# Fifteen tiles at the end of a fused cross network in another order, and the sixth group's output turned tile by tile

## The chip, the core and the metric

The kernel runs on one core of a Trainium2 chip. The metric is the device time of one execution in microseconds (us). Before the change the median of 3 runs was 473.92 us (473.2 to 474.08).

## The reference

A cross network of six layers over rows of 416 features (`B, F, D, L = 16384, 26, 16, 6`, all in bfloat16):

```python
x = x0
for l in range(L):
    proj = jnp.einsum('bd,de->be', x, ws[l]) + bs[l]
    x = x0 * proj + x
return x
```

Each layer is a 16384 x 416 by 416 x 416 product, a bias, a multiplication by the first input and an addition of the layer's own input. A row's layers depend on one another, the rows don't.

## The kernel before

**Groups, jobs, tiles, chunks.** The 16384 rows are cut into 8 groups (0 to 7) of 2048 rows. A job `(g, l)` is layer `l` of group `g`. Activations lie transposed, features on partitions: three full tiles of 128 features (`t` or `i` = 0, 1, 2) and a tail of 32. An output tile `((g, l), i)` has four chunks of 512 rows (`j` = 0 to 3). A chunk is 13 matmuls: on each of the four 32-row groups of the TensorE array one for each of the three input tiles, and one more for the 32 tail features on one of the row groups. A tile is so 52 matmuls of 32 x 128 weights over 512 columns (lines 1065 and 1069). The 32 tail features of the output of two or three jobs are computed together in a tail batch (`tails`, lines 689 and 677). Every chunk sums in a PSUM bank of its own, of which there are eight.

**Evacuation.** ScalarE adds the bias and writes the chunk to `tw` (line 551); for each pair of chunks VectorE multiplies by the first input (563) and adds the layer's input (568). The tail batch goes through lines 605 to 613. An addition is held back behind the next multiplication.

**Order.** `order` lists the 48 jobs; its last six are (5,5), (6,4), (7,3), (6,5), (7,4), (7,5). From the tenth job on nearly everything on TensorE is placed by a table, `ORDER`: `replay` reads it letter by letter, each letter naming one of the four row groups and which of the chunks begun lately it works on next, and `|` placing a tail batch. The table fits one order of tiles: with another order of tiles the whole table is a new one. `tiles` gives the order of tiles, and `where` after which tile a tail batch comes.

Called by their jobs, the last fifteen tiles that the table places are those of e5 = (5,5), d6 = (6,4), d7 = (7,3), e6 = (6,5) and e7 = (7,4). Before the change they stand so: e5 0, 1, 2; d6 0, 1, 2; d7 0, 1, 2; e6 0, 1; e7 0; e6 2; e7 1, 2. e6 needs d6, e7 needs d7. A tail batch for e5, d6 and d7 comes after d6 0, and one for e6 and e7 after e6 1; the planner may put either a little later.

**The last job** (7,5), "natural" in the code, is computed with the rows on partitions: 16 blocks of 128 rows, four at a time (`kk` = 0 to 3, in each of them `j` = 0 to 3), each with three matmuls over 128 features (line 1130), two small ones for tail and bias (1013, 1019), a copy by ScalarE (1176), a multiplication (1182) and an addition (1188) by VectorE, and a store (1195). The addition needs the layer's input, the output of e7, with the rows on partitions. It comes there in three ways: tile 0 and tile 1 by DMA transposes (`rest_turn`, line 935, tile 1 in two halves), tile 2 by TensorE transposes (`turn_last`, line 1141, two of them with a pair of chunks each) and copies (1150), the tail by TensorE (1155) and ScalarE (1163).

**Output of the other groups.** A group's output is turned into one buffer, `ost`, by DMA transposes (three tiles and the tail), then stored (line 923). There is only one `ost`: the turns of a group wait until the store of the group before has read it. All of these DMAs, the transposes of `rest_turn` and the small rotations of the tails (445, 446) are issued by SyncE, in the order of the program: one that waits holds up all behind it. Group 5 (the sixth) is turned by `turn(g, 0)` in `tails`, then, once all of e5 and its tail are done, by `turn_rest`, `turn(g, 1)` and `turn(g, 2)` in `output` (890, 897). Group 6 is turned tile by tile, each as soon as it is written (`turn_out`, 903, called in `finish_tile`); its tail's turn comes with the tail batch, its tail's copy into `ost` is ScalarE's (914), its two stores come late in the program.

Of the kernel before, what the change touches and what calls it, by code (L numbers as in the profile page):

```python
# [21 lines left out]
class Program:  # L22
# [179 lines left out]
READ, NEXT, BACK, SECOND, PAIR, TAILS, SUMS = 19, 56, 70, 92, 56, 220, 240  # L202
LETTERS = "ABCDEFGHIJKLMNOPQRSTUVWXYZabcdefghijklmnopqrstuvwxyz0123456789"
ORDER = (
    "ABCDMBCTNaELBaUfBWIfZSUHhKQPBCMTVIDSJATKBQLWBQXKNALCZQLWBQCbMRLWBITWBATWZMLCVYLSBQLCRbICRAPaJUeH"
    "N|AWPJQGDQBDWNITCJnQCZTIWBLQWNALWBQXCNIDWZIDWJYTCJbMWHRIODBMSBfICVDMSVIDSJAbeJMXCJgXSBQLOZDIWNTA"
    "CNTUBOQDNaTAJaDQZKXMSBPYCNbICVLQaBTIWNALWNQDKBAbWNITCBcPSIZDKRYXCRIPeBIXaNQLG|ABWPAVKPQBCPBUaPAN"
    "WbQdKHMVSDBQOXBMKXAVSLMBCPZQCPJAWfJQaHMVSDBQOXBMKXAVSLMBCPZAWPJAWfJYCLUZOTANaLUBSXNE|KDBUORDIDSB"
    "MfSBYfKRMXGAdPWAVKPQBaLQBTKNADOZTAaNAXKNYDWYJPCJbUCVTIBeQLBaTINWHAVODUKBXQKBLAVaQLGBAfWZATWJYPGA"
    "VPYBWPANWLYRCLBQWDNSLAJaQfBSMZLGQXBSI|CDVMCXBMeXQBKPAVeLMBafMVKTAhSLYNHCBQXBSMLBaAOXZQKHMVSDBQOX"  # L210
    "BMCbMVDOVISDBMeXANKfYROHAZWPANKfQBSLYNDKNAXCNQWDNAWbNISDYBSPUBKfMVCfMVSLEBaTMVCP|IBWLAVCXMRCPANe"
    "XYBKPVQaHNAaPBMbKRASLYNHCBQXNCMLWBAaPQVCLQBaTNIGfVQODNAPaJAXKQBLSBAOXYBWPQZCLZQOXFISDAVSDQNCfINS"
    "XBAXSNYGDAZSXINHeBYTCNYSLEBSfMVCP|IBWLAVCXMRCPANeXYBKPVQaHNAaPBMbKRASLYNHCBQXBSIPBaIDZSIDSZAbJSM"
    "XCJgXOBIWPBUKPAdWLMBKDZQXBOIDaVQLOBIbCVbQKNEDWBQWPBMCbMVDOVISDBUeTMJGXAVOfIRCLQBaTN|ECPBWAPBYOXB"
    "ULadAXSZMLGRDYSBQbKNALWBQXKBQDOZIDVaITOBIbOBAbORcHKVATWMJHCUBXCMRLWAJTWMBPKAZLCBYPeQJXGARPWIZHCQ"
    "BTaN|ECPBWAPBYOXBUPadQDOZIXSMBPKVALSBQbCNAPWZAXSJPYWBPUCNULSBITOZALWBUTCNQLCZAXaNQLWFATWARPKUBDO"
    "YBXaMJTCIZDSIZXOQFDaARXCQNXCINDaUJPCANebQBSLZMGXBUiTN|ECPVSALBUCXNQCPJAeZXAWTJMaHBYORDYKNTACNfQW"
    "BPISBbISNDYKPVAKXBQWLBQXKNALCZQWLBQCbNAWPJAeLUZSDQJObAJXOYBLOVAXKBULCVQKDRIaXFAWPBUOLRAKbNQCDNQW"
    "DJMSXFAOTBASPZUCPJUSjF|ASPVIGDBYDaNITCJQbOVEDWMBXCMRDaMJXSEBDWAdXSIBfSVYLOBIXORALORYDKBQXCMRDaJM"
    "XSBIPSVALCRUbKBQLWBITWNEDCZTUKBITWBIDaRULOBAbSdMLGBUbSJE|ODVPAKBYDWRIDSJAfSBcbKNQXGZAPWBUPKRALaB"  # L220
    "UTCNQLCZITWMBPWJADOVAXeNITGBYTCRYLWARDaNQXKBITWNALOBYXCNQLCZITWBQLWBITWBQLOVADOQZXCNITWFATOBYPKR"
    "ALaNQDCNQXKFATWBQPWBAPSZULGBAbWNQDOdYTWFM|BCTMXBWMLBWAPdWQKDJAWfIZODYJOXAJXOYBLOVAXKNQHCBQWDMRCb"
    "BMaTVICLBYWfJAXeQZKHVMSDBQOXANKXAVSLMBCPYRKXABaPQVHKARXaIBLCVYLSNEXCMBWPIBWLAVCXMBWPAdKXYNGDMVaT"
    "JACXYNeTJ|EODBTAOBcOXBUPeZQKHVASXIBKTAZLSUBCXNQCPIZWDQJWDIRWPEBfCURbOEBPWAVKPQBCPQVaLENCXBQWPANW"
    "LAVCXQBSPYBaLAZWLMRGbIBSXAdSLYNHCBQXBSIPBaIDZSIDSZIXBScXJO|AXKRMDCNQDaNITGBQbBaITBaQLVOALOVAXOBU"
    "PKBUDVOITGBDUeBQXOdEbJWM|RCLASXBMSDNYKTBAOXQZCLMRCbINeTUFOLABaPAVKPQBCPVAOXRAePJAaXcJOHURKPQFCDO"
    "TAB"
)


# [76 lines left out]
def bass_standalone__cross_network_dcn__recsys_kernel(  # L307
# [24 lines left out]
    batches = []  # L332
# [336 lines left out]
    def tails(batch, corners_last=False, banks=None):  # L669
        bs_ = banks or take(len(batch))  # L670

        def corners():
            for (g, l), b in zip(batch, bs_):
                s3, tok3 = x3_src(g, l)
                for j in range(NJ):
                    (ri, qi), (ro, qo) = quad(g, l, j), quad(g, l + 1, j)
                    add("pe", lambda h, l=l, b=b, s3=s3, ri=ri, qi=qi, ro=ro, qo=qo: h.matmul(  # L677
                        psum[qo, b * CH:(b + 1) * CH], w3[l][qi, NT * P:D], s3[qi, :],
                        start=not corners_last, stop=corners_last, tile_position=(ri * T32, ro * T32)),
                        reads=tok3 + [("w3", l, ri)], writes=[("ps", b)])  # L680

        if not corners_last:
            corners()
        for (g, l), b in zip(batch, bs_):
            src, stok = x_src(g, l)
            for t in range(NT):
                for j in range(NJ):
                    ro, qo = quad(g, l + 1, j)
                    add("pe", lambda h, t=t, j=j, src=src, l=l, b=b, ro=ro, qo=qo: h.matmul(  # L689
                        psum[qo, b * CH:(b + 1) * CH], wm[l][:, t, NT * P:D], src(t, j, j + 1),  # L690
                        start=(corners_last and t == 0), stop=(not corners_last and t == NT - 1),
                        tile_position=(0, ro * T32)),
                        reads=[stok(t, j), wm_tok(l, NT)], writes=[("ps", b)])
            if not corners_last:
                evacuate_tail(g, l, b)
        if corners_last:
            corners()
            for k in sorted(range(len(batch)), key=lambda k: k != 1):
                evacuate_tail(*batch[k], bs_[k], vector=k == 1)
                while behind_tail:  # L700
                    behind_tail.pop(0)()
        pr.flush()
        for g, l in batch:
            if (g, l) == (LAST - 2, L - 1):
                turn(g, 0)
        for g, l in batch:
            if corners_last:
                prefill(g, l + 1)
                filled.add((g, l + 1))
        for g, l in batch:  # L710
            if (g, l) == (LAST - 1, L - 1):
                turn_rest(g)
            done_with(g, l)
        while later:
            load_group(later.pop(0))
# [158 lines left out]
    def output(g):  # L874

        s, s3 = xset[(g, L)], xtail[(g, L)]
        if g < LAST - 1:
            if g < LAST - 2:
                turn(g, 0)
            turn_rest(g)  # L880
            spread("pool")
            turn(g, 1)
            turn(g, 2)
            store(g, 0, NJ)
        free_x.append(s)
        free_3.append(s3)

    def turn(g, t):
        s = xset[(g, L)]
        add("sp", lambda h: h.dma_start_transpose(  # L890
            ost[:, :, t * P:(t + 1) * P], xs[s][:, t * GC:(t + 1) * GC]),
            reads=[("x", s, t, j) for j in range(NJ)], writes=[("ost", t, j) for j in range(NJ)],
            lane="ot" if t else "ot0", batch=g)

    def turn_rest(g):
        s3 = xtail[(g, L)]
        add("sp", lambda h: h.dma_start_transpose(ot3[:, :, :], x3s[s3][:, :]),
            reads=[("x3", s3)], writes=["ot3"], lane="ot3", batch=g)

    def turn_out(g, t):  # L900
        s = xset[(g, L)]
        for j0, j1 in ((0, NJ),) if t < NT - 1 else ((0, 2), (2, NJ)):
            add("sp", lambda h, j0=j0, j1=j1: h.dma_start_transpose(  # L903
                ost[:, j0 * KK:j1 * KK, t * P:(t + 1) * P], xs[s][:, t * GC + j0 * CH:t * GC + j1 * CH]),
                reads=[("x", s, t, j) for j in range(j0, j1)], writes=[("ost", t, j) for j in range(j0, j1)],
                lane=f"ot_{t}{j0}", batch=g)
# [32 lines left out]

    items = []  # L940
    where = {(b[0 if b in batches[4:-3] else min(1, len(b) - 1)], 0): b for b in batches[:-1]}
    where[((LAST - 1, L - 1), 1)] = batches[-1]
    del where[((0, 0), 0)]
    where[((0, 1), 0)] = where.pop(((1, 0), 0))
    tiles = [((1, 0), 0), ((1, 0), 1), ((0, 1), 0), ((0, 1), 1), ((0, 1), 2), ((1, 0), 2)]
    tiles += [(jb, i) for jb in order[3:-3] for i in range(NT)]
    end6, end7 = order[-3:-1]
    tiles += [(end6, 0), (end6, 1), (end7, 0), (end6, 2), (end7, 1), (end7, 2)]
    for jb, i in tiles:
        items.append(("tile", jb, i))  # L950
        if (jb, i) in where:
# [167 lines left out]
    g, l = LAST, L - 1  # L1119
# [155 lines left out]
```

## Time and profile before

| | us |
|---|---|
| median of 3 runs | 473.92 |
| profiled execution | 473.04 |
| its span on the core | 471.2 |
| TensorE busy in the span | 457.5 |
| VectorE busy | 403.3 |
| ScalarE busy | 380.7 |

A row of a timeline or of the chain begins with the start and the length in us from the span's start; then come the engine (PE is TensorE's matmuls, PEld its weight loads, DVE VectorE, ACT ScalarE, POOL GpSimd, SPq the DMA queue that SyncE issues to), the line of the kernel, the operation, output and input, and how many were merged in the row. Square brackets hold the idle time before it and what ended that.

### The profile page before, as it was taken

To read this page: it belongs to the slowest core of one execution; us is meant where nothing else is said; L and a number is where in the kernel's file an instruction comes from. 1 tells how busy PE (TensorE), PEld (TensorE's weight loads), DVE (VectorE), ACT (ScalarE), POOL (GpSimd) and SP (SyncE) were. 2 spreads that over 40 slices of the span, in tenths; PEclk is the share of its full clock that TensorE was granted. 3 is DMA by queue.
4 is the path that set the end of the run, shared out by engine and by line. 5 is a ranking of instruction groups with operands and counts; after the bars stand their busy time and mean duration, and the time that the engine had idled before them with its cause. 6 is when DMAs were issued, how large, how long until landed. Compare 5 with 4: busy or idle time off the path is not lost.

```text
span 471.2 us, 17812 instructions
## 1 busy us (share of the span) xinstructions
PE 457.5 (97%) x7997; PEld 264.1 (56%) x8001; DVE 403.3 (86%) x696; ACT 380.7 (81%) x609; POOL 5.5 (1%) x15
## 2 busy tenths in 40 slices
PE   9999999999999999999999999999999999999990
PEld 5444656565555567555655656566665555555540
DVE  2897899889889899798989898888988989988956
ACT  4686888887988889798888888788898888887870
POOL 1000000000000000000000000000000000000000
PEclk9999999999999999999999999999999999999996
DMA  8986969000003939094488975940000490306799
GB/s 230 180 184 141 153 110 190 4 25 7 21 2 55 187 113 189 15 153 152 70 155 155 219 141 110 218 154 3 24 4 3 89 224 16 70 2 126 195 182 295
DMA packets 139088, 53.78 MB, mean 114 GB/s; under 512 B 112762, under 2 KB 138500, under 8 KB 139012
## 3 DMA queue, kind: packets, MB, share of 16 engines
q1 hardware_dynamic: 138856, 52.54, 52.8%
q8 instruction: 62, 1.02, 0.9%
q10 hardware_dynamic: 156, 0.11, 0.1%
q14 instruction: 14, 0.11, 0.1%
HBM read 5.97 MB, written 13.63 MB: 42 GB/s over the span
## 4 chain that ended last, share of the span: by engine, by line
PE 93%; DVE 4%; SPq 1%; DMA 1%; ACT 1%; issue 0%; DVEq 0%
PE ps L1065 71%; PE ps L689 7%; PE ps L1069 6%; PE ps L642 4%; PE ps L636 1%; PE ps L677 1%; DVE tw L563 1%; DVE x L1182 1%; DVE x L1188 1%; DVE x L568 1%; PE ps L769 1%; DMA x<-x 1%; ACT tw L551 1%; PE ps L787 1%; PE ps L663 1%; SPq L903 0%
## 5 line engine op out<-in xcount | busy, mean ns | idle before, releaser
L1065 PE MATMUL ps<-x,wm 32*128 32x512 bf16 x6288 | 372.4, 374 | 0.0
L551 ACT ACTIVATE tw<-ps,bias 128x512 bf16<-128x512 f32 x524 | 326.1, 687 | 50.2 <-PE ps L1065 39.2
L1065 PEld LDWEIGHTS ps<-x,wm 32*128 32x128 bf16 x6288 | 220.8, 92 | 136.0 <-ACT tw L551 6.1
L563 DVE TENSOR_TENSOR tw<-tw,x 128x1024 bf16<-128x1024 bf16 x262 | 176.6, 690 | 42.2 <-ACT tw L551 41.1
L568 DVE TENSOR_TENSOR x<-tw,x 128x1024 bf16<-128x1024 bf16 x262 | 170.2, 685 | 0.3
L1069 PE MATMUL ps<-x,w 32*128 32x512 bf16 x524 | 158.2, 374 | 0.0
L1069 PEld LDWEIGHTS ps<-x,w 32*128 32x128 bf16 x524 | 44.4, 92 | 6.9
L689 PE MATMUL ps<-x,wm 128*32 128x512 bf16 x564 | 33.6, 380 | 0.0
L609 ACT ACTIVATE ts<-ps,bias 128x512 bf16<-128x512 f32 x32 | 20.4, 685 | 12.4 <-PE ps L677 12.4
L515 ACT ACTIVATE tw<-ps,bias 128x1024 bf16<-128x1024 f32 (+1 forms) x24 | 20.7, 937 | 8.2 <-PE ps L663 7.0
L689 PEld LDWEIGHTS ps<-x,wm 128*32 128x32 bf16 x564 | 13.5, 96 | 18.3 <-ACT tw L551 3.7
L642 PE MATMUL ps<-x,wm 128*128 128x512 bf16 x88 | 20.4, 379 | 0.7 <-issue 0.5
L613 DVE TENSOR_TENSOR x<-ts,x 128x512 bf16<-128x512 bf16 x47 | 18.5, 418 | 0.4
L524 DVE TENSOR_TENSOR tw<-tw,x 128x1024 bf16<-128x1024 bf16 (+1 forms) x21 | 13.0, 636 | 2.2 <-ACT tw L515 2.1
L642 PEld LDWEIGHTS ps<-x,wm 128*128 128x128 bf16 x92 | 8.3, 97 | 11.4 <-issue 2.1
L605 DVE SCALAR_TENSOR_TENSOR ts<-ps,bias,x 128x512 bf16<-128x512 f32 x15 | 11.2, 746 | 2.5 <-PE ps L677 2.4
L611 DVE TENSOR_TENSOR ts<-ts,x 128x512 bf16<-128x512 bf16 x32 | 12.7, 416 | 0.0
L529 DVE TENSOR_TENSOR x<-tw,x 128x1024 bf16<-128x1024 bf16 (+1 forms) x21 | 12.6, 633 | 0.0
L1188 DVE TENSOR_TENSOR x<-x,x 128x832 bf16<-128x832 bf16 (+1 forms) x9 | 4.8, 542 | 6.5 <-DMA x<-x 6.3
L1130 PE MATMUL ps<-wm,x 128*128 128x416 bf16 x48 | 9.7, 340 | 0.0
L1176 ACT ACTIVATE x<-ps 128x416 bf16<-128x416 f32 x16 | 7.6, 518 | 1.8 <-PE ps L1130 1.7
L797 DVE COPY x<-ps 128x512 bf16<-128x512 bf16 x5 | 2.0, 422 | 8.2 <-PE ps L787 8.2
(50 smaller groups left out, 70.6 us busy)
## 6 DMA issues: line engine op xcount, KB each, us to landing
out_dram<-ost SPq DMA_DIRECT2D x6, 1664.0 KB, 7.5
x<-x SPq DMA_DIRECT2D x24, 96.0 KB, 2.1
x<-in_x_dram SPq DMA_DIRECT2D x8, 208.0 KB, 4.2
x<-in_x_dram SPq DMA_DIRECT2D x4, 416.0 KB, 8.2
out_dram<-ost SPq DMA_DIRECT2D x2, 832.0 KB, 5.3
wm<-in_ws_dram SPq DMA_DIRECT2D x5, 312.0 KB, 3.4
x<-x SPq DMA_DIRECT2D x22, 64.0 KB, 2.0
out_dram<-x SPq DMA_DIRECT2D x3, 416.0 KB, 4.7
```

The source lines that it names most:

```text
L515: add("act", lambda h, a=a, w=w, b0=b0: h.activation(tw[r][:, a * CH:(a + w) * CH], psum[:, b0 * CH:(b0 + w) * CH], ACT_F.Identity, bias=b ...
L524: add("dve", lambda h, a=a, e=e: h.tensor_tensor(tw[r][:, a * CH:e * CH], tw[r][:, a * CH:e * CH], x0s[s0][:, i * GC + a * CH:i * GC + e * ...
L551: add("act", lambda h: h.activation(tw[r][:, j * CH:(j + 1) * CH], bank(b), ACT_F.Identity, bias=bias[:, i, l:l + 1], scale=1.0), reads=[( ...
L563: add("dve", lambda h: h.tensor_tensor(tw[r][:, o], tw[r][:, o], x0s[s0][:, c], ALU.mult), reads=[("tw", r, k) for k in both] + [x0_tok(s0 ...
L568: add("dve", lambda h: h.tensor_tensor(xs[so][:, c], tw[r][:, o], src(i, a, a + 2), ALU.add), reads=[("tw", r, k) for k in both] + [stok(i ...
L609: add("act", lambda h: h.activation(ts[r][:, :], bank(b), ACT_F.Identity, bias=bias[:, 3, l:l + 1], scale=1.0), reads=[("ps", b), "bias"], ...
L611: add("dve", lambda h: h.tensor_tensor(ts[r][:, :], ts[r][:, :], x03, ALU.mult), reads=[("ts", r)] + tok0, writes=[("ts", r)], release=True)
L613: add("dve", lambda h: h.tensor_tensor(x3s[so][:, :], ts[r][:, :], res, ALU.add), reads=[("ts", r)] + rtok, writes=[("x3", so), ("x3", so, ...
L642: add("pe", lambda h, t=t, j=j: h.matmul(bank(banks[j]), wm[l][:, t, ecols], src(t, j, j + 1), start=(first and t == 0), stop=(not first a ...
L689: add("pe", lambda h, t=t, j=j, src=src, l=l, b=b, ro=ro, qo=qo: h.matmul(psum[qo, b * CH:(b + 1) * CH], wm[l][:, t, NT * P:D], src(t, j, ...
L1065: add("pe", lambda h, l=l, t=t, j=j, b=b, q=q, ecols=ecols, src=src, kw=kw: h.matmul(bank(b), wm[l][q, t, ecols], src(t, j, j + 1)[q, :], ...
L1069: add("pe", lambda h, l=l, b=b, q=q, ecols=ecols, s3=s3, kw=kw: h.matmul(bank(b), w3[l][q, ecols], s3[q, :], **kw), reads=tok3 + [("w3", l ...
```

## The change

The order of the last fifteen tiles, the place of the last tail batch, the way in which group 5's output is turned, and the table. The new order of tiles is e5 0; d6 0, 1, 2; e5 1, 2; e6 0; d7 0, 1, 2; e6 1, 2; e7 0, 1, 2. The last tail batch is listed after e6 2, the one before it still after d6 0.

```diff
 ORDER = (
-    "ABCDMBCTNaELBaUfBWIfZSUHhKQPBCMTVIDSJATKBQLWBQXKNALCZQLWBQCbMRLWBITWBATWZMLCVYLSBQLCRbICRAPaJUeH"
...
+    "ABCDMBCTNaELRWMDdCYPJWEfNSIjCJUDSJATKBQLCRIXCRULOBAPaRXICRDYOJTUGBAXaBXQCdTIOVHCcRPUCNXISBDUiRPI"
...
         pr.flush()
         for g, l in batch:
-            if (g, l) == (LAST - 2, L - 1):
-                turn(g, 0)
-        for g, l in batch:
             if corners_last:
                 prefill(g, l + 1)
                 filled.add((g, l + 1))
         for g, l in batch:
-            if (g, l) == (LAST - 1, L - 1):
+            if l == L - 1 and g > LAST - 3:
                 turn_rest(g)
             done_with(g, l)
...
         if g < LAST - 1:
             if g < LAST - 2:
                 turn(g, 0)
-            turn_rest(g)
+                turn_rest(g)
             spread("pool")
-            turn(g, 1)
-            turn(g, 2)
+            if g < LAST - 2:
+                turn(g, 1)
+                turn(g, 2)
             store(g, 0, NJ)
...
     def turn_out(g, t):
         s = xset[(g, L)]
-        for j0, j1 in ((0, NJ),) if t < NT - 1 else ((0, 2), (2, NJ)):
+        for j0, j1 in ((0, NJ),) if t < NT - 1 or g < LAST - 1 else ((0, 2), (2, NJ)):
...
-    where[((LAST - 1, L - 1), 1)] = batches[-1]
+    where[((LAST - 1, L - 1), 2)] = batches[-1]
...
-    tiles += [(jb, i) for jb in order[3:-3] for i in range(NT)]
-    end6, end7 = order[-3:-1]
-    tiles += [(end6, 0), (end6, 1), (end7, 0), (end6, 2), (end7, 1), (end7, 2)]
+    tiles += [(jb, i) for jb in order[3:-6] for i in range(NT)]
+    e5, d6, d7, e6, e7 = order[-6:-1]
+    tiles += [(e5, 0), (d6, 0), (d6, 1), (d6, 2), (e5, 1), (e5, 2), (e6, 0), (d7, 0), (d7, 1), (d7, 2),
+              (e6, 1), (e6, 2), (e7, 0), (e7, 1), (e7, 2)]
...
     def finish_tile(g, l, n=1, i=0):
         tiles_done[(g, l)] = tiles_done.get((g, l), 0) + n
-        if (g, l) == (LAST - 1, L - 1):
+        if l == L - 1 and g > LAST - 3:
             turn_out(g, i)
```

The instructions are the same in number and kind on every engine, except that group 5's turns are now issued at line 903's place in the code (901 in the changed kernel). On SyncE's queue the order from group 5's output on becomes: group 5 tile 0, four rotations, group 5 tail, group 5 tile 1, tile 2, group 5's store; group 6 tile 0, tile 1, the two halves of tile 2, its tail; `rest_turn` 0 and the two halves of `rest_turn` 1; group 6's two stores; the stores of group 7. Before, group 6's tail and tile 1 came in turn after its tile 0, then `rest_turn` 0, then the halves of group 6's tile 2, then those of `rest_turn` 1.

More of the change, by code (lines that the diff above doesn't have):

```diff
@@ L204 @@
 ORDER = (
-    "ABCDMBCTNaELBaUfBWIfZSUHhKQPBCMTVIDSJATKBQLWBQXKNALCZQLWBQCbMRLWBITWBATWZMLCVYLSBQLCRbICRAPaJUeH"
[L206 to L224, printed above, removed]
@@ L225 @@
-    "LAVCXQBSPYBaLAZWLMRGbIBSXAdSLYNHCBQXBSIPBaIDZSIDSZIXBScXJO|AXKRMDCNQDaNITGBQbBaITBaQLVOALOVAXOBU"
-    "PKBUDVOITGBDUeBQXOdEbJWM|RCLASXBMSDNYKTBAOXQZCLMRCbINeTUFOLABaPAVKPQBCPVAOXRAePJAaXcJOHURKPQFCDO"
-    "TAB"
+    "ABCDMBCTNaELRWMDdCYPJWEfNSIjCJUDSJATKBQLCRIXCRULOBAPaRXICRDYOJTUGBAXaBXQCdTIOVHCcRPUCNXISBDUiRPI"
+    "|CJXQCBPQWZLACVMfRaHUBOTUJCTIBaLQCZTAORAPaBXYODVOYTBKYBXQKZDQKZXMGRDMaBXCMRXCMRLCYJTAaRAPaJTUCRL"
+    "OUBLCYRXCMRDaMJDWYBXQKNbECBbQWdPIGRUDNCMDaNIXCJAbWRIDSJYDKBYfKVMTGBMbRWAPR|CPQKBDMWBXIORDcKZDUKR"
@@ new lines @@
+    "bMGJXAWJDQCNbAOJDYWRLMCJbUCRDMSJbEWNDUCNTICbJUCRLMWFDMWTBICVTICJDYWJTMCJDQaBbMShXEKN|DUKNAXCBQXO"
+    "BMLWBgXKZMTGVAPSVAPKQBDOURDOIRDKBfUSBfQKVbMGRLASBPQCZPAOJDYWJDUKZDUSBfQOJbECVbMKBLUSBTINCIDhSLUO"
+    "BXICRIXOBAPSYVDCUNbSFICTZUCPRICfJQWPF|IaDRLECBXCURPCMJDaUJPAWZPKQBLCURfAORLUCJTAaBPYSBPYKRXAdSPU"
+    "BOLCUZTAORLUCJTAaRDYSJPUGTBQCBXQOZLECVTAeRLOUFDUCRXANSDYCNbQWJDISBbcCRbMWIdHCYRXO|IBLWTIBCVDMSVD"
+    "MKBbIWNTYCNbAOZLUCJTAaRLUOBLUCRXAORLUCJTMWFDUORDMKBXAOBbUORLAKZTUCBTOYVLGQNDAeRXMKFDUCRXASNLUCJX"
@@ new lines @@
+    "AWBPUSJDcKBbUKdTMGVDMWLBICbVQK|ABPWTMBKZDAWZTOcJXQCJTASdLUOBLUCRXICRLUCJTMWBLAaVTMKFDUCVTASNAPJC"
+    "cbWBULSNYDKZMXSBIPRCIbNCULOBAPaRXAORDYOJTUCJDYSVDQKBbQKNfEWJDQCZPQKFDAWRjMCNLUCJXQOF|LAWRAPCNUDO"
+    "UJDWBXMKBfUKZDQVKbERCTAeNLUCJXMSBPICVDgOIBXaQJPCIZXOBIDSZUCPRICbQJOXAJWDQVCPQBObANWLQBTKMZfCZULS"
+    "NH|AOBXMCNDASZPWcBLOURbCINbUCVPISBLYSNALCRAbNSDYKNDYWJPQCJbASVbIOBLUCRLUCRXIBSDMRaLUCBbMVSDMRKbU"
+    "CRPIWBXICRLUCRLAaJAWbRATOJYDKBcXSJYHNCXMBOXIdCLQWNH|AOBXMCBTYCZTIWBTIWPZCIBTcWZLECVTcNCPIBaULBWI"
@@ new lines @@
+    "TCRAPZSUDJSAbRKUPFCMXBWIPRCIDRWgLBSIXNCIXNCULBSDMBebUKRPECZAbORAPaJTUCRLOcBLCYRXCMRLWAJCYXRATOBY"
+    "PeJUHRCPQKBIbCZQLWNH|AOBXMCNDMCZMXCNgXRaELBaQXJCQLBaITCZIDWBMXSJYDKZAbSVIPCJUbCRULOBIDaRIXCJTUCB"
+    "XMSZLEWNDCYRXANSLUCJXAWBPUSJDcKZQDSJbMCZMXCNIXBWQLN|GDMWBPICVDMSBYjSJMHCZMXKBIXSBQLCRLAShIXOFQDC"
+    "RUDSNIXGBQXCRMLWBAbSVIPCBYPBWYLNSAbdOAXZKQPGBYPSBIPCVYLORALOBAbORUDOJUDVCTUNCMfJWQDJSfMFWDMVCMXK"
+    "BIXSNALCRUDSNIXCBYXORELWBQDBSfUZKALZSXIG|BXQOJDYCZDMSJXAKBbQWNLYCBbUORLEChTAaRLUOBLUCRXAORLUCJTM"
@@ L228 @@
+    "WFDUCVTMKBDMaRXECBXYSNLECZXSARLYOBLUCRXIOBLUCBXQOZDINaDUZKPQCJbAWRbASJPUCJDYSBYTCNQbKdALaVQPGBMb"
+    "WBUPKRDI|RCTIOBLUCBbMWRDMKZTUCRDQaNXAKNQXCJMTWBAPCZXcKRPAaJUPGBUPCVIDeRULOFAXCRMXBCTYNCPIVCLUBiT"
+    "UJebERWLM|BCPQVCDQWNLAWJAXKBUfCNcTWZELORUDCNQXBOITBaQLNCAPZSAbJSUDRKUPFCAbRWMDJCgbJWQPFCMXBWMLZC"
+    "IDRaIXFODUCRXMBOAbNWLAVCUPBWcLBWIfNSYHVKMTBCMTZCIPBWIDRWAPKRYXGJMT|CBQPBaPIBCPUZCXICdTIaJPUSDAeV"
+    "TYB"
 )
```

## The prediction

> **What bounds the kernel now.** I read the counts of TensorE in the timeline first, to see whether the long middle has anything to give, then the chain of waits at the end, then SyncE's queue, which that chain runs into. The rows are the tail batches, which cut the table's stream into stretches whose matmuls can be counted in the order of instructions, and the first matmul of the last job.
>
> ```profile
> 57.91 2.13 PE L689 MATMUL ps<-x,wm 128*32 128x512 bf16 x36
> 90.50 2.13 PE L689 MATMUL ps<-x,wm 128*32 128x512 bf16 x36
> 391.21 2.13 PE L689 MATMUL ps<-x,wm 128*32 128x512 bf16 x36
> 419.02 2.13 PE L689 MATMUL ps<-x,wm 128*32 128x512 bf16 x36
> 447.28 0.88 PE L1130 MATMUL ps<-wm,x 128*128 128x416 bf16 x4
> ```
>
> From 391.21 to 419.02 lie 516 matmuls, so 27.81 / 516 = 53.9 ns each; from 57.91 to 90.50 lie 604, so 54.0 ns. The first stretch has no place where a row group of the array comes round sooner than every fourth matmul, the second has 13. So TensorE is paced evenly, with the tail batches included, and such places cost it nearly nothing (0.1 ns x 604 = 0.06 us for 13 of them). The last job's first matmul has the same number in both orders, 7909. I call its start T = 447.28. Nothing in the middle can be won, and T moves only if the new order stalls.
>
> After T the chain of waits reads so (start, length, what):
>
> ```profile
> 454.45 1.33 SPq L903
> ...
> 457.20 3.29 DMA x<-x
> ...
> 460.58 0.59 DVE x L1188
> ```
>
> The end hangs on the second half of `rest_turn` 1, issued at 457.20 and landed at 460.49, behind the halves of group 6's tile 2 (line 903) on the queue. The timeline of the end shows what it holds up:
>
> ```profile
> 444.79 4.15 ACT L551 ACTIVATE tw<-ps,bias 128x512 bf16<-128x512 f32 x7 [0.16 <-DVE x L568]
> 447.30 1.29 DVE L568 TENSOR_TENSOR x<-tw,x 128x1024 bf16<-128x1024 bf16 x2
> 448.21 1.31 PE L1130 MATMUL ps<-wm,x 128*128 128x416 bf16 x6
> 448.50 1.29 DVE L563 TENSOR_TENSOR tw<-tw,x 128x1024 bf16<-128x1024 bf16 x2
> 449.70 1.28 DVE L568 TENSOR_TENSOR x<-tw,x 128x1024 bf16<-128x1024 bf16 x2
> 450.45 0.62 PE L1141 MATMUL ps<-ident,x 128*128 128x128 bf16 x8 [0.93 <-DVE x L568]
> 451.70 0.52 PE L1130 MATMUL ps<-wm,x 128*128 128x416 bf16 x2
> 457.62 2.28 PE L1130 MATMUL ps<-wm,x 128*128 128x416 bf16 x12
> 458.36 2.10 ACT L1176 ACTIVATE x<-ps 128x416 bf16<-128x416 f32 x4 [0.58 <-PE ps L1130]
> 459.31 0.59 DVE L1188 TENSOR_TENSOR x<-x,x 128x832 bf16<-128x832 bf16 x1 [5.66 <-DMA x<-x]
> 466.80 0.65 DVE L1182 TENSOR_TENSOR x<-x,x 128x416 bf16<-128x416 bf16 x2
> 467.37 0.65 DVE L1188 TENSOR_TENSOR x<-x,x 128x416 bf16<-128x416 bf16 x2
> 468.05 0.39 ACTq L1195 DMA_DIRECT2D out_dram<-x  x1
> ```
>
> VectorE stands idle for 5.66 us for the DMA, then works off multiplications and additions until 467.37 + 0.65 = 468.02, while TensorE ended at 459.90 and ScalarE at 460.46. After the landing VectorE needs 468.02 - 460.58 = 7.44 us; from its last result to the span's end, a store, lie 471.2 - 468.02 = 3.18 us. Were the transposes early, the end would follow ScalarE's 460.46 instead.
>
> Why they are late is in SyncE's queue:
>
> ```profile
> 436.47 0.41 SPq L923 DMA_DIRECT2D out_dram<-ost  x1
> 443.75 1.74 SPq L903 DMA_TRANSPOSE ost<-x  x1
> 445.55 1.93 SPq L897 DMA_TRANSPOSE ot<-x  x1
> 447.53 3.06 SPq L903 DMA_TRANSPOSE ost<-x  x1
> 450.69 1.85 SPq L935 DMA_TRANSPOSE x<-x  x1
> 452.58 3.20 SPq L903 DMA_TRANSPOSE ost<-x  x2
> 455.83 2.71 SPq L935 DMA_TRANSPOSE x<-x  x2
> 458.71 1.13 SPq L923 DMA_DIRECT2D out_dram<-ost  x2
> ```
>
> Group 6's tile 0 goes out at 443.75, 7.28 us after group 5's store was issued, because that store had to leave `ost` first. From there the queue has no gap: eight transposes one after the other until 458.54.
>
> **The change part by part.** *The new places of the tiles.* Counting matmuls back from T at 53.9 ns gives the time of a tile's last chunk. How long from there to the written tile shows today's e7 1: its last chunk ends 28 matmuls before T, at 445.77, its additions at 447.30 + 1.29 = 448.59, so 2.8 us. In the new order e5 2 ends 487 matmuls before T (421.0), e6 1 216 (435.6), e6 2 175 (437.8), e7 0 79 (443.0) and e7 1 30 (445.7). Written they are at 423.8, 438.4, 440.6, 445.8 and 448.5.
>
> *Group 5's output.* Its landings are bounded by these rows, min, median and max of lines 890, 923 and 935, in this order:
>
> ```profile
> DMA to landing us min/median/max: 4.3/5.0/6.2
> DMA to landing us min/median/max: 4.3/7.4/8.6
> DMA to landing us min/median/max: 3.3/3.4/4.4
> ```
>
> Tile 2's turn goes out at 423.8 and lands at 428.8; the store follows and has left `ost` at 428.8 + 7.4 = 436.2, against 443.75 today. The wait for the store does not vanish, it ends 7.5 us sooner. Behind it stand group 6's turns: tile 0 from 436.2 to 437.9 (1.74), tile 1 from 438.4, when it is written, to 441.5 (3.06), the halves of tile 2 to 444.7 (3.20), the tail to 446.6 (1.93).
>
> *The tail in front of `rest_turn`.* The last tail batch moves behind e6 2: its last matmul is 105 before T, at 441.6. SyncE now waits for group 6's tail before `rest_turn` 0. In the rows below, after today's last batch (its last matmuls 433.80 + 0.41 = 434.21), VectorE begins with it at 434.31, and the second tile behind it is written at 439.79.
>
> ```profile
> 433.80 0.41 PE L677 MATMUL ps<-x,w 32*32 32x512 bf16 x8
> 434.31 0.75 DVE L605 SCALAR_TENSOR_TENSOR ts<-ps,bias,x 128x512 bf16<-128x512 f32 x1 [1.08 <-PE ps L677]
> 437.56 0.42 DVE L613 TENSOR_TENSOR x<-ts,x 128x512 bf16<-128x512 bf16 x1
> 439.11 1.28 DVE L568 TENSOR_TENSOR x<-tw,x 128x1024 bf16<-128x1024 bf16 x2
> ```
>
> Its second tail is written at 437.98, 3.8 us after the matmuls; so group 6's is there at 445.4 at the latest, and its turn ends between 446.6 and 447.3. The last job's own tail is first in VectorE's order and needed 58 matmuls (3.1 us) after the batch, against about 1.3 us of work: nothing.
>
> *`rest_turn`.* Tile 0 goes out until 448.5 to 449.2 (1.85), the two halves of tile 1 follow, the second 1.37 us after the first, at 449.9 to 450.6, and lands 3.3 us later at 453.2 to 453.9. With all the longest landings it is 456.9 (2.4 us later at group 5, less 0.5 us of slack before tile 1, and 4.4 instead of 3.3). Group 6's stores, issued behind it, cost nothing as long as they end before group 7's last one: today's pair goes out at 458.71 and is not in the chain.
>
> *What is late next: the last job itself.* Two things delay it. First, e6 0 now stands only 83 matmuls (4.5 us) behind the pair of d6 2 that it reads, with the batch of three tails just before on VectorE. Its reader comes 112 matmuls (6.0 us) after that batch. By the rows above VectorE needs 439.79 - 434.21 = 5.6 us for two tails and the tiles behind them, and a third tail adds 2 x 0.34 us: 6.3 us. That is a stall of 0.3 us; bounds 0 and 1.0, for the second pair can be late as well. Second, in e7 2 the chunks 2 and 3 now end before 0 and 1, and VectorE takes the pairs in that order, but line 1141's first transposes read pair 0, 1. Today that pair is the third of four operations and written at 450.4, and TensorE goes on at 450.45. Now it is the fourth, written between 450.98 and 451.3 (ScalarE's queue of seven ends at 448.94 today, 0.0 to 0.2 later then). From there to line 1130's next matmuls pass 1.25 us today, with a wait for the second pair inside, and about 1.1 us without. Delay 0.5 to 0.8 us, and I take 0.65; bounds 0 and 1.0.
>
> *The sum.* ScalarE's end 460.46 + 0.3 + 0.65 = 461.4. Behind its last copy stand three of VectorE's four last small operations; the four took 468.02 - 466.80 = 1.22, so 0.9 us, and the end is 462.3. VectorE keeps up with that if the second half lands before 462.3 - 7.44 = 454.9; expected are 453.2 to 453.9, so the wait is gone. The span ends at 462.3 + 3.2 = 465.5, 5.7 us less than 471.2. The profiled execution took 473.04, so 467.3; the median of the runs lies 0.9 above that execution, so 468.2 us.
>
> **The rivals.** *The queue is still late.* For it speaks that the whole queue has only 1.0 to 1.7 us of slack (454.9 less 453.2 to 453.9) and a store's landing has been as long as 8.6. Against it, that 7.5 us are gained where it starts. With the longest landings the half lands at 456.9, 2.0 us past 454.9: 470.2 us.
>
> *The clock drops (slower).* In the gap before line 1141 TensorE now waits from 448.21 + 1.31 = 449.52 to 451.1 or later, 1.6 to 1.9 us instead of 0.9. The last stretch of the span shows that idle time costs clock (PEclk is the number after the engines' busy times):
>
> ```profile
> 460.00:471.20 11.20, 0.00 (x0) 0.00 (x0) 7.26 (x16) 0.46 (x1) 0.00 (x0) 0.61 0.98 298
> ```
>
> The last matmul ended at 459.90; if the clock then stays full and falls to a half, a mean of 0.61 over 11.2 us puts the fall at 460.0 + 0.22 x 11.2 = 462.5, 2.6 us after it. Should the gap reach that length, the matmuls from 451 on, 8.5 us up to 459.9, would take up to twice as long: 468.2 + 8.5 = 476.7 us. It decides from a gap of 2.6 us on, that is, if e7 2 were written 0.7 us later than my latest. [...]
>
> *The new table stalls somewhere.* All of the stream is in another order. Per nanosecond of pace the 7,524 matmuls from the table's start to T cost 7.5 us. Against it: the shortest distance from a pair's last chunk to its first reader in the stream is 83 matmuls in both orders, and the places where a row group comes back early are 87 instead of 76, by the price above 0.05 us. A loss of 0.4 ns makes 3.0 us and 471.2 us; from 0.76 ns on all is given back.
>
> *It does not do what it says.* If e5's later tiles pushed the store out to where it is today, the chain would be the old one: 473.9 us. e5 2's count, 26 us before T, speaks against it.
>
> **How the numbers follow.** Forecast 0.80; queue late 0.10; table 0.05; clock 0.03; no effect 0.02. With the bounds of the two delays (0 to 2.0 in place of 0.95) the forecast's own range is 467.2 to 469.3; measuring adds some 0.5 on both sides, and the late queue (470.2) and most of the table's case up to 471.2 are taken in: 466.7 to 471.2. Faster by over 0.2% (about 0.95 us, what a measurement tells from no change) 0.93, within it 0.03, slower 0.04.
>
> **What would show it.** VectorE's idle time before line 1188 (1187 after the change) falls from 5.66 us to under 1; group 5's store goes out near 428.8 and group 6's tile 0 near 436; the second half of `rest_turn` 1 lands near 453.5; the last job's first matmul stays within 0.5 of 447.3, and line 1141 begins near 451.4; the chain's end goes over TensorE and ScalarE (1130, 1176) to VectorE. The prediction is wrong if a DMA still precedes the first addition by more than a microsecond, if T has moved by more than 1 us, or if the granted clock falls before 460.

## The result, and the profile after

| | before | after |
|---|---|---|
| median of 4 runs each, us | 473.72 | 470.23 |
| lowest to highest, us | 473.2 to 474.08 | 469.75 to 471.47 |

The ratio is 0.9931, with a 95% interval of 0.9909 to 0.9953: 3.5 us faster, where 5.7 were forecast. The time lies inside the range (466.7 to 471.2), 2.0 us above the forecast, at the value that the rival of the late queue gave (470.2).

The execution that was profiled first is the slowest of the four (471.47, span 469.7), and two things are in it that none of the nine other profiles has: the table's stream started about 1 us late (41.81 us, elsewhere 40.46 to 40.87), because TensorE waited 1.05 us, until 22.21, for a load of the input, and the clock fell before the last matmul, to 0.50 at 454.3 us. A second profile of the same kernel, called a2_changed below, has neither (470.41, median of its six runs 470.20), and is the one to compare by sums. In the changed kernel line 903 is 901, 935 is 933, 1130 is 1129, 1141 is 1140 and 1188 is 1187.

SyncE's queue in the first profile after the change (start, length, line, how many merged):

```profile
424.03 5.93 SPq L901 DMA_TRANSPOSE ost<-x  x2
432.29 0.41 SPq L921 DMA_DIRECT2D out_dram<-ost  x1
440.55 8.71 SPq L901 DMA_TRANSPOSE ost<-x  x4
449.31 2.13 SPq L895 DMA_TRANSPOSE ot<-x  x1
451.53 5.13 SPq L933 DMA_TRANSPOSE x<-x  x3
```

The store of group 5 goes out 4.2 us sooner than before (432.29, was 436.47), and group 6's first turn behind it 3.2 us sooner (440.55, was 443.75). What the new order was to give stands there: the queue is earlier, but it still has no gap from 440.55 to 456.66.

The gap of TensorE in the last job, the wait of VectorE for the second half of `rest_turn` 1, and VectorE's last additions, from the timelines of these two engines:

```profile
449.61 0.88 PE L1129 MATMUL ps<-wm,x 128*128 128x416 bf16 x4
450.55 1.26 PE L1129 MATMUL ps<-wm,x 128*128 128x416 bf16 x6
453.70 0.62 PE L1140 MATMUL ps<-ident,x 128*128 128x128 bf16 x8 [1.90 <-DVE x L568]
```

```profile
458.75 0.59 DVE L1187 TENSOR_TENSOR x<-x,x 128x832 bf16<-128x832 bf16 x1 [0.55 <-DMA x<-x]
...
465.75 0.65 DVE L1187 TENSOR_TENSOR x<-x,x 128x416 bf16<-128x416 bf16 x2
```

Before the change VectorE waited for the DMA twice: the 5.66 us that the prediction shows are the wait for the first half of `rest_turn` 1, and the second half, on which the end hung, cost 0.68 more:

```profile
460.58 0.59 DVE L1188 TENSOR_TENSOR x<-x,x 128x832 bf16<-128x832 bf16 x1 [0.68 <-DMA x<-x]
```

Here the first of the two waits is gone and the second is 0.55. In its stead TensorE waits 1.90 us ahead of line 1140, where it waited 0.93. And in this one execution the granted clock (the number behind the five pairs of busy time and count) fell after that gap:

```profile
454.00:455.00 1.00, 1.00 (x11) 0.70 (x9) 0.64 (x1) 0.39 (x1) 0.00 (x0) 0.65 1.13 209
455.00:456.00 1.00, 1.00 (x10) 0.71 (x7) 0.24 (x2) 0.53 (x2) 0.00 (x0) 0.50 1.09 211
456.00:457.00 1.00, 1.00 (x10) 0.14 (x8) 1.00 (x2) 0.85 (x2) 0.00 (x0) 0.50 0.94 180
457.00:458.00 1.00, 1.00 (x8) 0.40 (x5) 0.89 (x2) 0.08 (x1) 0.00 (x0) 0.65 1.10 204
```

From two means of 0.65 between 1 and 0.5 follows a fall at 454.3 and a return at 457.7: 3.4 us at half the clock. The chain of waits of this execution therefore ends over TensorE and ScalarE (start, length, what):

```profile
453.70 0.62 PE ps L1140 x8
...
462.51 0.65 PE ps L1129 x3
...
463.71 0.53 ACT x L1175
...
464.67 0.59 DVE x L1187
```

That is the chain which was forecast, but for a reason that was not: TensorE is at half speed in it. The experiments ask which of the two holds the usual execution: the queue, or TensorE's gap with the clock behind it.

### The profile page after: what moved, and what is told of

Same layout as the page of the kernel before. It is cut to its first block, busy times and chain, and to the rows that moved or that the text cites. A ratio compares the mean times of both kernels' runs of the same rounds, so it can differ in the third digit from the quotient of the medians.

```text
span 469.7 us, 17812 instructions
## 1 busy us (share of the span) xinstructions
PE 460.1 (98%) x8001; PEld 262.5 (56%) x8001; DVE 404.8 (86%) x696; ACT 380.8 (81%) x609; POOL 6.6 (1%) x15
## 4 chain that ended last, share of the span: by engine, by line
PE 92%; SPq 3%; DVE 2%; DMA 1%; ACT 1%; issue 0%; DVEq 0%; ACTq 0%
PE ps L1064 72%; PE ps L689 6%; PE ps L1068 6%; PE ps L642 3%; SPq L408 2%; PE ps L1129 1%; PE ps L677 1%; DMA x<-in_x_dram 1%; ACT tw L551 1%; PE ps L636 1%; SPq L729 1%; DVE tw L563 1%; DVE x L568 0%; SPq L413 0%; SPq L401 0%
## 5 line engine op out<-in xcount | busy, mean ns | idle before, releaser
L1068 PE MATMUL ps<-x,w 32*128 32x512 bf16 x524 | 155.4, 374 | 0.0
L914 POOL COPY ost<-ot 128x512 bf16<-128x512 bf16 x6 | 5.2, 860 | 414.6 <-DMA ot<-x 414.6
```

Source lines behind the costliest of these rows:

```text
L1068: add("pe", lambda h, l=l, b=b, q=q, ecols=ecols, s3=s3, kw=kw: h.matmul(bank(b), w3[l][q, ecols], s3[q, :], **kw), reads=tok3 + [("w3", l ...
```

## The experiments

All ran beside the kernel before, in two jobs. Its median was 473.37 us in the first job and 473.34 in the second.

| run | job | median, us | ratio | 95% |
|---|---|---|---|---|
| e1_own | 1 | 467.83 | 0.9886 | 0.9872 to 0.9899 |
| e2_warm | 1 | 470.09 | 0.9927 | 0.9915 to 0.9940 |
| e5_own_warm | 1 | 467.78 | 0.9885 | 0.9871 to 0.9898 |
| e3_tilewise_only | 1 | 468.63 | 0.9895 | 0.9881 to 0.9910 |
| a2_changed | 2 | 470.20 | 0.9930 | 0.9910 to 0.9949 |
| e4_order_only | 2 | 470.23 | 0.9926 | 0.9911 to 0.9942 |
| e6_tilewise_own | 2 | 467.59 | 0.9872 | 0.9852 to 0.9891 |
| e7_own_pairs | 2 | 467.37 | 0.9868 | 0.9851 to 0.9884 |

### e1_own: the wait for the store taken away

Group 5's output gets a buffer of its own, a slot of first inputs that no group reads any more. By the program, group 6's turns then don't wait for group 5's store. Everything else is the changed kernel.

```diff
...
+    own5 = x0s[so][:, 0:XW + CH].rearrange("p (a f) -> p a f", f=D)
...
+    def oview(g):
+        return own5 if g == LAST - 2 else ost
...
-                ost[:, j0 * KK:j1 * KK, t * P:(t + 1) * P], xs[s][:, t * GC + j0 * CH:t * GC + j1 * CH]),
+                oview(g)[:, j0 * KK:j1 * KK, t * P:(t + 1) * P], xs[s][:, t * GC + j0 * CH:t * GC + j1 * CH]),
...
```

> The changed kernel, but group 5's output has a buffer of its own (the first inputs of group 4, no longer needed), so that group 6's turns do not wait for group 5's store. Theory Q (the queue still sets the end: the second half of rest_turn 1 landed at 458.72 and VectorE needs 7.4 us from there): the half lands about 3.4 us sooner against the last job's first matmul, VectorE's wait for a DMA is gone, and 1.5 us are gained on the changed kernel: 468.7 us. Theory C (the end is set by TensorE, whose clock falls to 0.50 for 3.4 us after the longer gap): the wait is gone as well, but the clock still falls and the time stays at 470.2 us. Both in one: a gain where the clock does not fall, none where it does.

Measured: 467.83 us, 2.4 us less than the changed kernel, where theory Q had 1.5. Its queue and VectorE's first and last rows of the last job:

```profile
430.93 0.41 SPq L936 DMA_DIRECT2D out_dram<-x  x1
431.39 14.04 SPq L916 DMA_TRANSPOSE ost<-x  x4
445.47 1.28 SPq L910 DMA_TRANSPOSE ot<-x  x1
446.85 5.74 SPq L948 DMA_TRANSPOSE x<-x  x3
```

```profile
453.13 1.49 DVE L1164 COPY x<-ps 128x1024 bf16<-128x1024 bf16 x2 [0.72 <-PE ps L1155]
...
462.94 0.65 DVE L1202 TENSOR_TENSOR x<-x,x 128x416 bf16<-128x416 bf16 x2
```

Group 6's first turn is issued right behind the store (431.39) and not 8 us later. The store is in its way all the same: this one turn, the first of the four in the second row, stays on SyncE's queue for 7.47 us, until 438.86, and the store lands at about 439.2. The second turn goes out at 439.33, where the changed kernel's first does (439.38 in the profile of a2_changed). So the queue is ahead by little more than one turn, and `rest_turn` is through at 452.59, 3.1 us sooner than in a2_changed. That is enough: no row of VectorE after 453.13 waits for a DMA, and it works from there to 463.59, 10.46 us without a pause of note. The queue was what held the changed kernel; without its lateness VectorE's own work in the last job is the bound.

### e2_warm and e5_own_warm: the clock kept up

Six more matmuls on constants in TensorE's gap, into a bank that the transposes behind them overwrite; e2 in the changed kernel, e5 in e1.

```diff
...
+    keep_busy(24, b2)
     turn_last(0, b2)
...
```

> The changed kernel with six matmuls of 128 x 512 on constants more (1.3 us) in the gap of 1.9 us ahead of the last tile's transposes; their result is overwritten. Theory C: the clock stays at 1.00, the last job's TensorE part is 1.7 us shorter, and the time falls to 468.5 us. Theory Q: the clock stays up, but the end is held by the landing of rest_turn 1, VectorE's wait in front of line 1187 grows from 0.55 to about 2 us, and the time falls by 0.2 to 0.5 us only: about 469.9 us, with less spread between the runs.

> Both edits together. If queue and clock hold the end side by side, this gains what neither does alone: VectorE's wait gone, the clock at 1.00, 468.3 us (1.7 to 2.2 less than the changed kernel). If only one of them counted, it equals the better of the two single ones.

Measured: 470.09 against 470.20 to 470.23 for the changed kernel, and 467.78 against 467.83 for e1. In e2 VectorE waits 0.50 and 0.83 us for the two halves, where theory Q had about 2. In its profile the granted clock stays at 1.00 to the last matmul. A clock that is kept up is worth nothing in the median, so the fall in the first profile doesn't explain the missing 2 us. The clock of a2_changed, over the stretch in which the first profile's had fallen, says the same:

```profile
453.00:459.00 6.00, 6.00 (x56) 3.11 (x53) 4.27 (x8) 4.47 (x10) 0.00 (x0) 1.00 1.06 248
```

### a2_changed: the changed kernel once more

> The changed kernel itself once more, timed beside the following ones, for a second profile. If the later start of the first profile (the first matmul of the last job at 449.6) was that execution's own, it now stands near 448.4, as in the three kernels built on it, and the time stays at 470.2 us. If the clock's fall is not in every execution, this profile shows it or not; in either case the second half of rest_turn 1 lands about 9 us after the last job's first matmul and VectorE waits for it where the clock stays up.

Measured: 470.20 us, six runs from 469.3 to 472.04. Its queue, then VectorE's waits for the two halves and its end, then TensorE's gap, then the place in the chain of waits where the queue enters it:

```profile
425.93 2.88 SPq L901 DMA_TRANSPOSE ost<-x  x1
...
431.18 0.41 SPq L921 DMA_DIRECT2D out_dram<-ost  x1
439.38 8.41 SPq L901 DMA_TRANSPOSE ost<-x  x4
447.84 2.58 SPq L895 DMA_TRANSPOSE ot<-x  x1
450.51 5.14 SPq L933 DMA_TRANSPOSE x<-x  x3
```

```profile
456.46 0.59 DVE L1187 TENSOR_TENSOR x<-x,x 128x832 bf16<-128x832 bf16 x1 [0.48 <-DMA x<-x]
457.73 0.59 DVE L1187 TENSOR_TENSOR x<-x,x 128x832 bf16<-128x832 bf16 x1 [0.68 <-DMA x<-x]
...
464.52 0.65 DVE L1187 TENSOR_TENSOR x<-x,x 128x416 bf16<-128x416 bf16 x2
```

```profile
448.69 0.88 PE L1129 MATMUL ps<-wm,x 128*128 128x416 bf16 x4
...
452.78 0.62 PE L1140 MATMUL ps<-ident,x 128*128 128x128 bf16 x8 [1.90 <-DVE x L568]
```

```profile
454.31 3.32 DMA x<-x
...
457.73 0.59 DVE x L1187
```

Here, at full clock, the chain goes over the DMA: the second half of `rest_turn` 1, landed at 457.63. From the addition that waits for it to VectorE's end are 464.52 + 0.65 - 457.73 = 7.44 us, the same 7.44 as before the change. The end still hangs on that landing; it only comes 2.85 us sooner (457.73, was 460.58).

The end hangs on the queue in a second way. Group 6's two stores stand right behind `rest_turn` on it (the first goes out at 455.82), and together with group 7's stores they write 3328 KB. By the trace the DMA engines move 327 to 337 GB/s in every microsecond from 457.6 to 466.6, and the last packet ends 1.0 us before the span does. VectorE's last result is followed by 468.6 - 465.17 = 3.4 us. In e1, where group 6's stores go out at 452.78, the rate falls to about 220 GB/s from 460.8 to 462.8, so these engines have time to spare, and behind VectorE's end come only 465.8 - 463.59 = 2.2 us. Before the change and in e2, e3, e4 and e6 the engines write to the end without a pause as well. So the output's writing and VectorE's work end side by side in the changed kernel, both behind one queue; no run here takes them apart.

### e3_tilewise_only and e4_order_only: the two parts alone

e3 is the kernel before, in its order of tiles and with its table; only group 5's output is turned tile by tile.

```diff
...
-            if (g, l) == (LAST - 1, L - 1):
+            if l == L - 1 and g > LAST - 3:
                 turn_rest(g)
...
-        if (g, l) == (LAST - 1, L - 1):
+        if l == L - 1 and g > LAST - 3:
             turn_out(g, i)
...
```

> The kernel before, its order of tiles and its table untouched, with only group 5's output turned tile by tile. Theory T (the gain is the earlier store of group 5, whatever the order): the store goes out near 430.2 instead of 436.5, group 6's tile 0 near 437.5, the second half of rest_turn 1 lands at 454 to 456, and the end follows ScalarE with TensorE's gap at 0.9 us and the clock at 1.00: 467.3 to 469.3 us, as good as the changed kernel or better. Theory O (the order of tiles is what counts, since e6's tile 2 stands in front of rest_turn 1 in this order): at most 1 us is gained, 472.7 us or more.

Measured: 468.63 us, 4.7 less than before and 1.6 less than the changed kernel (1.5 less than e2, which ran in the same job). Its queue, TensorE's gap, and VectorE's wait and end:

```profile
407.67 8.30 SPq L901 DMA_TRANSPOSE ost<-x  x3
...
426.11 2.15 SPq L895 DMA_TRANSPOSE ot<-x  x1
430.39 0.41 SPq L921 DMA_DIRECT2D out_dram<-ost  x1
438.65 3.26 SPq L901 DMA_TRANSPOSE ost<-x  x1
```

```profile
447.42 0.88 PE L1128 MATMUL ps<-wm,x 128*128 128x416 bf16 x4
...
450.60 0.62 PE L1139 MATMUL ps<-ident,x 128*128 128x128 bf16 x8 [0.93 <-DVE x L568]
```

```profile
456.37 0.59 DVE L1186 TENSOR_TENSOR x<-x,x 128x832 bf16<-128x832 bf16 x1 [0.70 <-DMA x<-x]
...
463.16 0.65 DVE L1186 TENSOR_TENSOR x<-x,x 128x416 bf16<-128x416 bf16 x2
```

With the old order the store goes out at 430.39, 6.1 us sooner than before, without a tile moved: the three tiles are turned from 407.67 on, and the store waits for the tail's turn alone, issued at 426.11. Before, tiles 1 and 2 were turned behind that tail, where the program had put them. The last job starts at 447.42 and its gap is still 0.93 us.

The end doesn't follow ScalarE, as theory T had it: the second half of `rest_turn` 1 lands at 456.27, VectorE waits 1.27 and 0.70 us for the halves, and from there to its end are 7.44 us once more (463.81 - 456.37). That VectorE goes on 1.36 us sooner than in a2_changed comes from the queue, which starts 0.73 us sooner (438.65, there 439.38) and whose eight transposes take 15.68 us in this order and 16.27 in the new one.

e4 is the other part alone: the new order and table, group 5's output turned as before. It undoes the same hunks in the changed kernel.

> The changed kernel with group 5's output turned as before (tile 0 in the tail batch, the rest behind its tail when e5 is complete): order and table alone. Theory S (in the new order group 5's store waits for e5's tile 2, whichever way the rest is turned): nothing changes, 470.2 us, group 5's store near 431 as in the changed kernel. Theory T (the gain of the changed kernel is the tile-by-tile turn): the gain is lost, 473 us.

Measured: 470.23 us, the changed kernel's time. Its queue is the changed kernel's too:

```profile
431.06 0.41 SPq L923 DMA_DIRECT2D out_dram<-ost  x1
439.31 8.48 SPq L903 DMA_TRANSPOSE ost<-x  x4
```

In the new order e5 2's turn can't go out before about 425.9, when the tile is written (425.93 in a2_changed), and the store not before it has landed, wherever the program issues it. So each part does the same thing, an earlier store (at 430.4 by the one, at 431.1 by the other), and together they do it once.

### e6_tilewise_own: e3 with the buffer of its own

The edits of e3 and e1 on the kernel before.

> The kernel before, order and table untouched, with group 5's output turned tile by tile and in a buffer of its own. Theory Q: group 6's tile 0 goes out at 437.3, when it is written, instead of 438.65; the second half of rest_turn 1 lands near 455 instead of 456.3; with TensorE's transposes at 450.6 and VectorE then busy for 10.4 us without a wait the end is 1.3 us sooner than with the tile-by-tile turn alone: 467.2 us. If the order of the transposes in the queue (group 6's tile 2 in front of rest_turn 1) holds the end instead, it stays at 468.6.

Measured: 467.59 us, where theory Q had 467.2. Its queue, and VectorE's wait for the second half:

```profile
430.36 0.41 SPq L936 DMA_DIRECT2D out_dram<-x  x1
437.34 1.81 SPq L916 DMA_TRANSPOSE ost<-x  x1
```

```profile
454.93 0.59 DVE L1201 TENSOR_TENSOR x<-x,x 128x832 bf16<-128x832 bf16 x1 [0.60 <-DMA x<-x]
```

Group 6's tile 0 goes out at 437.34, when it is written. That is 1.3 us sooner than in e3, and the gain over e3 (in the other job) is 1.0 us. So the buffer of its own is worth 1.0 us in the old order, where tile 0 is written only 1.3 us before it could go out anyway, and 2.4 us in the new one (e1), where it was ready about 8 us before (431.39, not 439.38). VectorE is not without a wait here, as theory Q had it: it still waits 0.60 us for the second half and needs 7.45 us from there (462.38 - 454.93). In the old order the queue still holds the end.

### e7_own_pairs: the pair that is there first, read first

e1, and the last job's transposes of tile 2 begin with chunks 2 and 3, which in the new order are written first; the blocks of rows and their PSUM banks are taken in the matching order.

```diff
...
-    turn_last(0, b2)
-    turned_out(0, b2)
-    for j in range(NJ):
-        if j == 2:
-            turn_last(2, b3)
+    turn_last(2, b2)
+    turned_out(2, b2)
+    for j in (2, 3, 0, 1):
+        if j == 0:
+            turn_last(0, b3)
...
```

> The changed kernel with group 5's own buffer, and the last job takes the pair of chunks first that VectorE finishes first (2, 3 instead of 0, 1). Theory P (the turned order of the pairs costs 0.6 us): TensorE's transposes begin 0.6 us sooner, 3.5 instead of 4.1 us after the last job's first matmul, and the time falls by 0.6 against the own buffer alone: 467.2 us. If VectorE's work behind the landing decides, it stays at 467.8.

Measured: 467.37 us, the fastest of all, 0.46 less than e1 (in another job, with intervals that overlap). TensorE's gap and VectorE's end:

```profile
448.36 0.88 PE L1144 MATMUL ps<-wm,x 128*128 128x416 bf16 x4
...
451.84 0.62 PE L1155 MATMUL ps<-ident,x 128*128 128x128 bf16 x8 [1.29 <-DVE x L568]
```

```profile
462.43 0.65 DVE L1202 TENSOR_TENSOR x<-x,x 128x416 bf16<-128x416 bf16 x2
```

The gap is 0.61 us shorter than the 1.90 of the changed kernel and VectorE ends at 463.08, 0.51 sooner than in e1, with the last job's start at the same place to 0.01 us (e1's is at 448.37). So the order of the pairs costs the new order about 0.5 us.

## Why the prediction was right, and where it was not

**The direction and the queue: right. The end of the chain: not.** What held the end was the landing of `rest_turn` 1 behind group 6's turns behind group 5's store, and the change moved that landing forward, by 2.85 us. But the forecast had VectorE's wait gone and the end behind TensorE and ScalarE. In a2_changed VectorE still waits for both halves (0.48 and 0.68 us) and the chain still goes over the DMA; e1 shows that the queue is what holds it. Of the three signs by which the prediction called itself wrong, one came in every profile with the new order: the last job's first matmul stands at 448.32 to 449.61, over 1 us behind 447.28. The second, a clock that falls before 460, came in one profile; the third, more than a microsecond of DMA wait ahead of the first addition, did not come (0.48). The time lies inside the range because the range took in the rival of the late queue.

**Its last job starts later (T): mis-sized.** Forecast was a stall of 0.3 us at e6 0, and no more in the stream. From the first matmul of the table to the last job's first, e3, which has the old order, takes 447.42 - 40.62 = 406.80 us:

```profile
40.62 0.83 PE L1063 MATMUL ps<-x,wm 32*128 32x512 bf16 x12
```

a2_changed, with the new order, takes 448.69 - 40.87 = 407.82:

```profile
40.87 0.83 PE L1064 MATMUL ps<-x,wm 32*128 32x512 bf16 x12
```

and in the view of its waits (us in total, times, longest) the weight loads wait so for VectorE, where the old order has 0.4 us in two waits on line 605 and none on line 568:

```profile
PEld ps L1064 <- DVE ts L605: 0.8, 2, 0.6
...
PEld ps L1064 <- DVE x L568: 0.5, 1, 0.5
```

The longest of the first kind, and the second, stand in the timeline of the weight loads:

```profile
94.33 0.11 PEld L1064 LDWEIGHTS ps<-x,wm 32*128 32x128 bf16 x7 [0.55 <-DVE ts L605]
...
420.09 0.11 PEld L1064 LDWEIGHTS ps<-x,wm 32*128 32x128 bf16 x6 [0.49 <-DVE x L568]
```

The new order costs 1.0 us in the stream. Set matmul against matmul with e3, it is 0.6 us behind by 96 us, most of that (0.46) around the wait at 94.33, right after a tail batch, where TensorE wants the PSUM bank of a tail that VectorE has not read yet. The wait at 420.09 is the stall at e6 0, 518 matmuls ahead of T: the loads wait 0.49 us, but the stream falls back by 0.2 us only, so the forecast's 0.3 was about right. The other 0.2 us come behind it. What the forecast missed is so the rival of the table, at about a quarter of its price (0.8 of 3.0 us); the prediction looked at the distance of tiles and not at that of banks behind a tail batch.

**Group 5's output: right in kind, late by 2.1 us.** Set against the start of the last job, which takes the 1.0 us and the different starts out, the steps of the queue went so (forecast T is 447.28 + 0.3 = 447.58; measured is a2_changed, T = 448.69):

| us from T | forecast | measured |
|---|---|---|
| e5 2's turn issued | -23.8 | -22.8 |
| store issued | -18.8 | -17.5 |
| group 6's tile 0 issued | -11.4 | -9.3 |
| group 6's turns through | -2.9 | -0.9 |
| its tail through | -1.0 to -0.3 | +1.7 |
| second half of `rest_turn` 1 landed | +5.6 to +6.3 | +8.9 |

So 1.0 us is e5 2 written later than by the rule of 2.8 us behind its last chunk: it took 3.9 (425.90 - 422.02). The 2.8 came from a tile ahead of which VectorE had been idle for 0.70 us; here VectorE works without a pause from the tail batch on. 0.3 is its turn's landing (5.25 instead of 5.0), 0.8 the store's landing, 8.2 instead of 7.4. The 7.4 was a median over all stores of the run. From the issue of this store to the turn behind it pass 8.20 us in a2_changed and 8.25 or 8.26 in the first profile, in e4 and in e3, against 443.75 - 436.47 = 7.28 before the change. The traces' DMA packets point at an instruction load of 16 KB. In all nine profiles with the sooner store such a load begins 5.7 to 6.3 us behind the store's issue and takes 0.9 to 1.0 us (in the first profile 438.00 to 438.96); the last 3 to 18 packets of the store start when it ends, to 0.03 us, after a pause of 0.26 to 0.71 us. Before the change the load began 6.4 us behind the issue, and no packet of the store started after it. The size fits the missing 0.9 us, but no run was made for it. The 8.6 that the prediction gave as the longest was nearer.

**The turns and the tail: right for the turns, late by 0.65 for the tail.** Four turns took 8.41 against 8.5 with the pause that was expected. The tail's turn took 2.58 instead of 1.93, and the three of `rest_turn` 5.14 instead of 1.85 + 2.71 = 4.56.

**`rest_turn` and the limit: here the forecast fell.** The limit, 454.9 or T + 7.3, was right: VectorE needed 7.44 us behind the landing. The half landed 1.6 us behind it, where 1.0 to 1.7 us of slack were worked out. The delays stand one behind the other on one queue, so they add up, and their sum was larger than the slack. The rival "the queue is still late", with a chance of 0.10, is what happens. That its price, 470.2, agrees to a tenth is luck: it was summed from the longest landings of all, while the last half landed after 3.3 us as in the forecast, the later T and the longer transposes are not in it, and it holds 0.9 us for the step to the median that did not come.

**The sum, by its terms.** The span of a2_changed is 3.1 us longer than the forecast 465.5: 0.41 for the start of the table, 0.7 for the stream (1.0 less 0.3), 1.76 for VectorE's end (T + 16.48, forecast T + 14.72) and 0.2 for the stretch from there to the span's end. Against that stands the step from one profiled execution to the median: 0.9 was added, and for a2_changed it is -0.2 (470.41 to 470.20). 468.2 + 3.1 - 1.1 = 470.2.

**Group 6's stores: not free.** They were to cost nothing as long as they end before group 7's last store. In a2_changed the DMA engines write without a pause from group 6's stores to the end, and the stretch behind VectorE's end is 3.4 us, in e1 2.2. The 3.2 of the sum came from a kernel with the queue late, so it had this cost in it, though the forecast wanted the queue early.

**The pairs of e7 2: at the end of its bounds.** Forecast delay 0.65, bounds 0 to 1.0; line 1140 began 4.09 us behind T, line 1141 before the change 450.45 - 447.28 = 3.17: 0.92. In the median this is hidden behind the queue, and e7 shows that it counts where the queue is out of the way.

**VectorE keeps up: nearly.** e1 has no wait for the queue and ends 463.59 - 448.37 = 15.22 us behind T, 0.5 later than the 14.72 of the forecast; in e7 it is 14.72. So the forecast's time for the last job was right for a kernel whose pairs come in time. Its chain was not: in e1 and e7 the end goes over VectorE, which works without a pause, and not over TensorE and ScalarE.

**The clock: a fall was possible, at another length and price.** It was put at a gap of 2.6 us and 8.5 us. In the first profile it fell after a gap of 1.90 us. The price there, seen from T, is 466.40 - 449.61 - 16.48 = 0.3 us at the end, because the queue was late as well. e2 shows no price in the median. The 2.6 us were read off one fall, behind the last matmul; the last section has four such falls, 2.3 to 3.2 us behind it.

**The table's rival and "it does not do what it says": not so, and half so.** The store did go out sooner. But e4 shows that one of the change's two means to that end did nothing beside the other, and this the prediction didn't ask.

## What to carry to other kernels

When several DMAs stand one behind the other on a queue with the end behind them, work out the slack with the longest case of each step, of writing, issue and landing alike, and not with medians over the whole run: here five delays of 0.3 to 1.0 us, all of one sign, used up the slack of 1.0 to 1.7 us and 1.6 us more. Where a change has two means to one end, price each alone: the small edit in the old order gave 4.7 us, the new order, with its new table, 3.1, and both together no more than the order. A second buffer brought the old order to 467.59 us and the new one to 467.83. It takes the program's wait away and not the queue's: the turn that was issued right behind the running store held SyncE's queue for 7.47 us in e1. In the new order the next bound behind it was VectorE's work in the last job; in the old one VectorE still waited 0.60 us for the DMA.

## What was not expected of the hardware

**The clock fell with matmuls already running again.** In the first profile the last matmul ahead of the gap ended at 450.55 + 1.26 = 451.81, work resumed at 453.70, and the clock fell at 454.3, 2.5 us after the gap's beginning, for 3.4 us. The same gap of 1.90 us is in the profiles of a2_changed, e4 and e1, with a granted clock of 1.00 from 453 to 459 in all three. So one profile of four shows the fall, and the length of the gap alone doesn't decide it.

After shorter gaps at that place the clock stayed at 1.00: 0.93 us before the change and in e3, 1.29 us in e7. Behind the last matmul, where no other follows, it fell 2.3 us after that matmul's end in e1 (461.92 to 464.2), 2.4 in e3 (460.05 to 462.4), 2.5 before the change (459.91 to 462.38) and 3.2 in the first profile (464.72 to 467.95). In a2_changed and e7 it still stood at 1.00 at 465, 2.8 and 3.7 us behind it. So in these profiles no one length of idle time parts the falls from the rest. What sets the one execution with a fall after 1.90 us apart from the three without is not shown.

**Stalls in the stream repeat to 0.02 us.** From the table's first matmul to T the new order took 407.82 us in a2_changed, 407.80 in the first profile, 407.81 in e4; the old one 406.82 before the change and 406.80 in e3. Differences between executions come from the start (40.46 to 41.81 us until the table begins) and from the landings at the end.
